# Scale and bias of the exponential moved to VectorE for the last pair of heads, and a tile cleared in six pieces instead of three

## The chip, the cores and the metric

The kernel runs on one core of one Trainium2 chip. The metric is the device time of one execution in microseconds (us), as the median of several runs. A profile of one further execution shows what each engine did. The engines are called TensorE (PE in the profile; its weight loads are PEld), VectorE (DVE), ScalarE (ACT), GpSimd (POOL) and SyncE (SP).

## The reference

Three layers are computed one after the other, all in float32: attention in which a query sees only the keys of its own hash bucket, a mixture of eight experts with one expert for each token, and an ELU feed-forward layer.

```python
# q, k, v: (2, 8, 768, 64); 6 hash bits from the sign of q @ proj and k @ proj
scores = scale * np.matmul(q, k.transpose(0, 1, 3, 2))
scores = np.where(mask, scores, -1000000000.0)
scores = scores - np.max(scores, axis=-1, keepdims=True)
attn = np.exp(scores)
attn = attn / (np.sum(attn, axis=-1, keepdims=True) + 1e-09)
x = np.matmul(attn, v)                      # reshaped to 1536 tokens x 512
logits = x @ w_gate                         # e_idx = argmax; softmax weight of it
eom = 1.0 / (1.0 + np.exp(-(x @ w_output_gate)))
out[mask] = gate_w[mask, None] * eom[mask, e, None] * (np.maximum(x[mask] @ w1[e], 0.0) @ w2[e])
h = out @ w_in                              # 512 x 2048
return np.where(h > 0.0, h, np.exp(np.minimum(h, 0.0)) - 1.0) @ w_out
```

## The kernel before, in words

The order of the instructions on every engine is the order in which the code issues them; nothing reorders them.

The attention is one software pipeline of 96 row blocks (`NQ = 96`): 16 heads in 8 pairs, six blocks of 128 query rows for each head. Step `n` of the loop over `n` issues the stages of several blocks at once, in this order:

- `stage_M(n - 1)`: VectorE reduces the 128x768 scores of block n - 1 in PSUM to the negated row maximum `nm` (L369). GpSimd makes of it the scale `sc` (L370: 2 to the 64th where the row has a key in its bucket, else 0) and the bias `bi = sc * nm` (L371).
- `lows_t`: VectorE forms the low half of the second three transposed tiles of the block before (L405).
- `stage_A(n)`: GpSimd adds up the two halves of an earlier output (L431).
- `early`: what earlier steps have put off, all on VectorE here: the sum into `osb` (L447) for two of the later half heads, and the products of the joining step with the reciprocals of the sums (L509, L528).
- `stage_T(n - 3)`: TensorE transposes the probabilities of block n - 3 in two groups of three (L400) into three PSUM tiles that are used in turn; ScalarE rounds each group to its high half (L402), VectorE subtracts for the low half of the first (L407; the second waits as a `lows_t` for the next step). Between them VectorE may take the reciprocals of sums (L468).
- `stage_G`: GpSimd adds a small constant to the sums (L460).
- `stage_S(n)`: TensorE computes the scores of block n in four matmuls (L351) into one of two PSUM tiles.
- `stage_R`: TensorE joins two heads to token rows (L501).
- `stage_V`: TensorE multiplies the transposed probabilities of three blocks with v, four matmuls a step (L421), into the only PSUM tile `o`.
- `stage_E(n - 1)`: ScalarE computes the exponential with `bi` and `sc` as operands (L378), and with it the row sums.
- `stage_O`: ScalarE copies the finished output out of `o` (L446 and others).
- then whatever the list `todo` holds for step n, put there by `at(n, ...)`.

The last pair of heads are the blocks n = 84 to 95. While they run, the tokens of the first batch element go to their experts: `gate_first` puts its gate arithmetic on the steps 63 to 87 and six scatters (L638, an indirect DMA that GpSimd issues) on the steps 85, 87, 88, 90, 91 and 93. Each is followed on GpSimd by a one-element memset (`spacer`, L651). In step 96 SyncE loads the rows of the first expert.

The tile `zt0` holds zeros. GpSimd clears it early in the pipeline; from step 22 on SyncE writes it to the first rows of each expert's region (`zero_rows`).

Behind the attention come the experts (64 pieces of weights, streamed) and the feed-forward layer; the change touches neither.

Of the kernel before, what the change touches and what calls it, by code (L numbers as in the profile page):

```python
# [13 lines left out]
ALU = mybir.AluOpType  # L14
# [5 lines left out]
UNIT = float(2.0 ** 64)  # L20
# [5 lines left out]
def kernel(  # L26
# [19 lines left out]
    nc = tc.nc  # L46
# [21 lines left out]
    XC = DM + 16  # L68
# [82 lines left out]
    zt0 = ap1.tile([128, XC], F32, name="zt0")  # L151
# [187 lines left out]
    def tile_of(n):  # L339
        m, i = divmod(n, HALF)  # L340
        hd, hf = part_of(m)
        return hd, HALF * hf + i
# [19 lines left out]
    def stage_M(n):  # L362
        hd, c = tile_of(n)
        if c == 0:
            sums[hd] = ap2.tile([128, NC], F32, tag="sums", name="sums", bufs=3)
        nm = ap2.tile([128, 1], F32, tag="nm", name="nm", bufs=3)
        bi = ap2.tile([128, 1], F32, tag="bi", name="bi", bufs=3)
        sc = ap2.tile([128, 1], F32, tag="sc", name="sc", bufs=3)
        nc.vector.tensor_reduce(nm, sps[n][:, :, 0:HC], AX.XY, ALU.max, negate=True)  # L369
        nc.gpsimd.tensor_scalar(sc, nm, 0.25, UNIT, ALU.is_lt, ALU.mult)  # L370
        nc.gpsimd.tensor_tensor(bi, sc, nm, ALU.mult)  # L371
        soft[n] = (bi, sc)

    def stage_E(n):
# [347 lines left out]
    NQ = NH * NC  # L722
# [5 lines left out]
    def at(n, f, *a):  # L728
        todo.setdefault(n, []).append((f, a))
# [37 lines left out]
    for hh in range(2):  # L767
        at(10 + 2 * hh, joining_rows, rw, hh)
        at(14 + 4 * hh, joining_rows, rw_end, hh)
    for j in range(3):  # L770
        at(13 + 3 * j, nc.gpsimd.memset, zt0[:, j * XC // 3:(j + 1) * XC // 3], 0.0)
    for hh in range(2):
        at(12 + 3 * hh, load_gates, hh, False)
        at(61 + 3 * hh, load_gates, hh, True)
# [62 lines left out]
    for pc in range(E * NP):  # L837
        stream.append((pc,))
        j, i = divmod(pc - W2P, 7)
# [165 lines left out]
    for n in range(NQ + 3):  # L1005
# [4 lines left out]
        if 1 <= n < NQ + 1:  # L1010
            stage_M(n - 1)
# [491 lines left out]
```

## Time and profile before

| | us |
|---|---|
| median of 3 runs | 704.16 |
| lowest and highest | 703.58, 704.34 |
| the profiled execution | 704.39 |
| its span from first to last instruction | 702.3 |

The profiled execution took 2.1 us more than its span. TensorE's granted clock was 0.997 of full speed over the span. Durations and times below are from that one execution; times count from the start of the span. An instruction's start to the next one's start is its slot: instructions of an engine overlap a little, so a slot can be shorter than the duration. In a timeline a bracket at the end of a line tells the engine's idle time before it and what ended it.

### The profile page before, as it was taken

The numbers are of one execution on the slowest core, as the hardware profiler recorded it, in microseconds if no ns is written. First come the engines' busy times: TensorE is split into PE (matmuls) and PEld (weight loads), VectorE is DVE, ScalarE is ACT, GpSimd is POOL, SyncE is SP. The second block draws the span as 40 slices with busy tenths as digits, with TensorE's granted clock in tenths as the row PEclk, the third lists the DMA queues.
The fourth block names the chain that finished last, engine by engine and source line by source line (L and its number), as shares of the span: only waits on it lengthen the run. The fifth ranks groups of instructions, "written<-read, shape, count | busy, mean of one in ns | idle before, by whom it ended". The sixth has DMA issues, their size and how long they took to land.

```text
span 702.3 us, 12093 instructions
## 1 busy us (share of the span) xinstructions
PE 688.6 (98%) x4120; PEld 616.4 (88%) x4121; DVE 553.1 (79%) x1026; ACT 427.8 (61%) x854; POOL 214.6 (31%) x503
## 2 busy tenths in 40 slices
PE   8999999999999999999999999999999999999996
PEld 5799999999999989999999998888888888888885
DVE  6999999999999897888888898877788447934433
ACT  5998998999888767666766664444543224422221
POOL 5676556555566640221235410000000000002012
PEclk9999999999999999999999999999999999999998
DMA  8747658667572259777788984222122000001011
GB/s 194 195 115 210 173 161 203 181 174 203 148 201 79 77 184 327 237 244 251 229 211 229 264 218 113 93 88 91 61 90 91 0 1 0 1 1 60 7 53 64
DMA packets 47476, 96.92 MB, mean 138 GB/s; under 512 B 11752, under 2 KB 23848, under 8 KB 47408
## 3 DMA queue, kind: packets, MB, share of 16 engines
q1 hardware_dynamic: 44944, 89.67, 45.2%
q0 software_dynamic: 2304, 6.40, 2.4%
q8 instruction: 35, 0.57, 0.3%
q14 instruction: 33, 0.27, 0.1%
q10 hardware_dynamic: 160, 0.00, 0.0%
HBM read 63.68 MB, written 10.72 MB: 106 GB/s over the span
## 4 chain that ended last, share of the span: by engine, by line
PE 52%; issue 34%; DMA 6%; DVE 5%; ACT 2%; POOL 1%; SPq 0%; DVEq 0%; POOLq 0%; ACTq 0%
PE hps L1186 12%; PE s L351 8%; PE yps L1199 8%; PE o L421 8%; PE t L400 7%; DMA out_dram<-part,tidt 5%; PE yps L1201 3%; PE sp L501 2%; DVE nm L369 2%; PE zps L280 1%; PE xTp L1168 1%; DVE ptlo L407 1%; DMA qb<-qhi 1%; DMA tidt<-tid_d 1%; PE xacc L944 1%
## 5 line engine op out<-in xcount | busy, mean ns | idle before, releaser
L378 ACT ACTIVATE p<-s,bi,sc 128x768 f32<-128x768 f32 x96 | 95.8, 998 | 4.7 <-POOL bi L371 4.3
L886 DVE TENSOR_TENSOR wl<-wraw,wh 128x1024 fp32r<-128x1024 f32 (+1 forms) x65 | 77.2, 1190 | 21.8 <-ACT wh L882 19.6
L1344 POOL DMA_INDIRECT out_dram<-part,tidt x12 | 11.5, 959 | 265.4 <-DVE part L1341 264.2
L369 DVE TENSOR_REDUCE nm<-s 128x1 f32<-128x768 f32 x96 | 90.6, 944 | 2.0 <-POOL vst L330 1.1
L1306 ACT ACTIVATE ee<-gps 128x512 f32<-128x512 f32 x48 | 28.7, 597 | 100.1 <-PE gps L1296 100.1
L402 ACT ACTIVATE pthi<-t 128x384 fp32r<-128x384 f32 x192 | 84.0, 493 | 7.6 <-PE t L400 6.3
L1199 PE MATMUL yps<-h,wh 128*128 128x448 f32 x256 | 84.5, 380 | 0.0
L400 PE MATMUL t<-ident,p 128*128 128x128 f32 x576 | 80.3, 273 | 2.0 <-DVE ptlo L405 1.1
L1296 PE MATMUL gps<-x2l,vh 128*128 128x512 f32 x192 | 75.9, 395 | 0.0
L1326 PE MATMUL a<-vh,gl 128*128 128x512 f32 x192 | 75.8, 395 | 0.0
L1296 PE MATMUL gps<-x2h,vl 128*128 128x512 f32 x192 | 75.7, 394 | 0.0
L1296 PE MATMUL gps<-x2h,vh 128*128 128x512 f32 x192 | 75.7, 394 | 0.0
L1326 PE MATMUL a<-vh,gh 128*128 128x512 f32 x192 | 75.5, 393 | 0.0
L1326 PE MATMUL a<-vl,gh 128*128 128x512 f32 x192 | 75.5, 393 | 0.0
L351 PE MATMUL s<-ka,qa 128*128 128x384 f32 x192 | 73.3, 383 | 1.8 <-DMA qa<-qlo 1.2
L400 PEld LDWEIGHTS t<-ident,p 128*128 128x128 f32 x576 | 68.1, 140 | 7.8 <-PE t L400 1.5
L1307 DVE TENSOR_SCALAR ee<-ee 128x512 f32<-128x512 f32 x48 | 20.4, 426 | 68.0 <-ACT ee L1306 67.9
L1309 ACT ACTIVATE gh<-ee 128x512 fp32r<-128x512 f32 x48 | 30.4, 633 | 69.0 <-DVE ee L1308 69.0
L421 PE MATMUL o<-pthi,vst 128*128 128x384 f32 x192 | 66.9, 348 | 0.3
L882 ACT ACTIVATE wh<-wraw 128x1024 fp32r<-128x1024 f32 x63 | 66.2, 1052 | 0.0
L351 PE MATMUL s<-kb,qb 82*128 82x384 f32 x192 | 65.2, 340 | 0.0
L421 PE MATMUL o<-ptlo,vst 128*128 128x384 f32 x192 | 64.9, 338 | 0.0
(238 smaller groups left out, 1783.9 us busy)
## 6 DMA issues: line engine op xcount, KB each, us to landing
wraw<-in_moe_w_t_dram SPq DMA_DIRECT2D x64, 512.0 KB
w<-in_moe_w_in_dram SPq DMA_DIRECT2D x16, 512.0 KB
w<-in_moe_w_out_dram SPq DMA_DIRECT2D x16, 512.0 KB
ka<-khi SPq DMA_DIRECT2D x30, 192.0 KB
xs_d<-zt SPq DMA_DIRECT2D x8, 528.0 KB
xs<-xs_d SPq DMA_DIRECT2D x7, 462.0 KB
raw_v<-in_v_dram SPq DMA_DIRECT2D x8, 384.0 KB
kb<-klo SPq DMA_DIRECT2D x15, 192.0 KB
```

What stands on the lines that cost most here:

```text
L351: nc.tensor.matmul(ps[:, j, 0:HC], opnd[st, "q" + x][0:n1, cb], opnd[st, "k" + x][0:n1, j * HC:(j + 1) * HC], start=(x == "a"), stop=(x == ...
L369: nc.vector.tensor_reduce(nm, sps[n][:, :, 0:HC], AX.XY, ALU.max, negate=True)
L378: nc.scalar.activation(p.rearrange("p (a b) -> p a b", a=2), sps.pop(n)[:, :, 0:HC], AF.Exp, bias=bi, scale=sc, accum_out=sums[hd][:, c:c ...
L400: nc.tensor.transpose(ps[:, a, :], p[:, kt * 128:(kt + 1) * 128], ident)
L402: nc.scalar.activation(ho, ps, AF.Copy)
L421: nc.tensor.matmul(ops[m], vst[hd][:, kt, :], t[:, kt, :], start=(kt == 0 and x == 0), stop=(kt == NC - 1 and x == 1))
L882: eng_hi.activation(hi, r, AF.Copy)
L886: fs = [lambda c=slice(j, j + h): eng.tensor_tensor(lo[:, c], r[:, c], hi[:, c], ALU.subtract) for j in range(0, PW, h)]
L1186: nc.tensor.matmul(ps, w[:, dc, fs], x[:, dc], start=(i == 0), stop=(i == len(terms) - 1))
L1199: nc.tensor.matmul(ps, wh[:, f], h[:, :, f], start=(f == 0), stop=last)
L1296: nc.tensor.matmul(ps, w[:, dc], x[:, dc, th * TC:(th + 1) * TC], start=(dc == 0 and i == 0), stop=(dc == KD - 1 and i == 2),)
L1326: nc.tensor.matmul(ps, x[:, cs], w, start=(fb in first_fb and i == 0), stop=(fb in last_fb and i == 2))
```

## The change

Two edits. In `stage_M` the engine of the scale and of the bias is VectorE where n is 84 or more, and GpSimd as before elsewhere. The arithmetic is the same. The tile `zt0` (528 columns) is cleared in six pieces of 88 columns at steps 11, 12, 14, 15, 17 and 18, instead of three of 176 columns at steps 13, 16 and 19.

```diff
         nc.vector.tensor_reduce(nm, sps[n][:, :, 0:HC], AX.XY, ALU.max, negate=True)
-        nc.gpsimd.tensor_scalar(sc, nm, 0.25, UNIT, ALU.is_lt, ALU.mult)
-        nc.gpsimd.tensor_tensor(bi, sc, nm, ALU.mult)
+        eng = nc.vector if n >= NQ - 12 else nc.gpsimd
+        eng.tensor_scalar(sc, nm, 0.25, UNIT, ALU.is_lt, ALU.mult)
+        eng.tensor_tensor(bi, sc, nm, ALU.mult)
         soft[n] = (bi, sc)
...
-    for j in range(3):
-        at(13 + 3 * j, nc.gpsimd.memset, zt0[:, j * XC // 3:(j + 1) * XC // 3], 0.0)
+    for j in range(6):
+        at(11 + 3 * j // 2, nc.gpsimd.memset, zt0[:, j * XC // 6:(j + 1) * XC // 6], 0.0)
```

## Rows read from the trace of the kernel before

**Rows 1.** The page: the span, and each engine's busy time
```profile
span 702.3 us, 12093 instructions
PE 688.6 (98%) x4120; PEld 616.4 (88%) x4121; DVE 553.1 (79%) x1026; ACT 427.8 (61%) x854; POOL 214.6 (31%) x503
```

**Rows 2.** Windows: length, then busy us (instructions) by engine, clock, DMA share, GB/s
```profile
30.00:60.00 30.00, 30.00 (x201) 28.99 (x200) 28.14 (x52) 28.38 (x63) 21.30 (x64) 1.00 0.62 153
...
210.00:220.00 10.00, 9.87 (x65) 9.25 (x64) 9.49 (x18) 8.95 (x21) 7.38 (x20) 1.00 0.16 60
```

**Rows 3.** Waits, 209 to 235 us: total us, times, longest
```profile
PEld o L421 <- DVE osb L447: 0.9, 2, 0.5
...
ACT p L378 <- POOL bi L371: 0.3, 1, 0.3
PEld s L351 <- ACT p L378: 0.2, 1, 0.2
```

**Rows 4.** Chain of waits in order of time: start us, us, what
```profile
211.47 1.22 POOL xs_d L638
...
213.35 1.08 ACT p L378 x2
...
214.97 0.57 DVE osb L447
...
218.27 1.07 POOL xs_d L638
...
224.56 0.82 PE sp L501 x6
```

**Rows 5.** Timeline of TensorE: start us, us, engine, line, operation, out<-in
```profile
210.17 0.42 PE L351 MATMUL s<-ka,qa 128*128 128x384 f32 x1
...
212.25 0.42 PE L351 MATMUL s<-ka,qa 128*128 128x384 f32 x1
...
215.12 0.34 PE L351 MATMUL s<-kb,qb 82*128 82x384 f32 x1
215.58 0.44 PE L421 MATMUL o<-pthi,vst 128*128 128x384 f32 x1
```

**Rows 6.** Timeline of VectorE, the last pair of heads
```profile
209.25 0.95 DVE L369 TENSOR_REDUCE nm<-s 128x1 f32<-128x768 f32 x1
...
215.56 0.56 DVE L407 TENSOR_TENSOR ptlo<-t,pthi 128x384 fp32r<-128x384 f32 x1
216.03 0.95 DVE L369 TENSOR_REDUCE nm<-s 128x1 f32<-128x768 f32 x1
216.90 0.55 DVE L405 TENSOR_TENSOR ptlo<-t,pthi 128x384 fp32r<-128x384 f32 x1
...
225.53 0.55 DVE L405 TENSOR_TENSOR ptlo<-t,pthi 128x384 fp32r<-128x384 f32 x1
225.99 0.25 DVE L509 TENSOR_TENSOR lp<-sp,ri 128x96 f32<-128x96 f32 x1
226.15 0.55 DVE L528 TENSOR_TENSOR xw<-sp,ri 128x384 f32<-128x384 f32 x1
...
234.56 0.93 DVE L369 TENSOR_REDUCE nm<-s 128x1 f32<-128x768 f32 x1
```

**Rows 7.** Timeline of VectorE, the last gate
```profile
247.18 0.18 DVE L622 TENSOR_REDUCE g_zs<-g_oz 128x3 f32<-128x24 f32 x1
247.28 0.17 DVE L618 TENSOR_REDUCE g_se<-g_ed 128x3 f32<-128x24 f32 x1
247.48 0.31 DVE L620 TENSOR_SCALAR g_se<-g_se 128x3 f32<-128x3 f32 x1
```

**Rows 8.** Timeline of GpSimd, the first piece of the tile of zeros
```profile
41.37 0.24 POOL L1040 MEMSET zt<- 128x176 f32 x1
```

**Rows 9.** Timeline of GpSimd, a scatter beside the last gate
```profile
246.85 0.96 POOL L638 DMA_INDIRECT xs_d<-xw,g_idx  x1 [0.21 <-issue]
```

**Rows 10.** Groups by line on VectorE: busy us, mean ns, then idle before
```profile
L620 DVE TENSOR_SCALAR g_se<-g_se 128x3 f32<-128x3 f32 x2 | 0.5, 232 | 0.0
```


## The prediction

> **What bounds the kernel now.** I first read the page's busy shares. TensorE is busy 688.6 of 702.3 us, VectorE 553.1, GpSimd only 214.6 [rows 1]. So GpSimd can cost time only where something waits for it in line, and work given to VectorE is free only where VectorE has gaps. The whole-run average doesn't say whether it has any here. I therefore read the windows of the last pair of heads, whose twelve row blocks (n = 84 to 95) are reduced from 209.25 us on. In 210 to 220 us VectorE is busy 9.49 of 10 us and TensorE 9.87 [rows 2]. Two engines are nearly full at once. The reader should see that the engine that is to be relieved (GpSimd, 7.38 of 10) is the emptiest of the three, and that the work goes to one of the full ones.
>
> The table of waits for 209 to 235 us prices what GpSimd does wrong there: ScalarE's exponential waits for `bi` once, 0.3 us; TensorE then waits 0.2 us for the exponential, and twice, 0.9 us together, for the combined output `osb` (L447) [rows 3]. The chain of waits shows that these belong together: a scatter of 1.22 us at 211.47, behind it in GpSimd's queue the scale and bias, then the exponential at 213.35, then `osb` at 214.97; the same again behind the scatter at 218.27 [rows 4]. On TensorE's side the last matmul of L351 starts at 215.12 and takes 0.34, and the first of L421 starts only at 215.58, with the end of `osb` at 215.54 [rows 4, 5]. So what the change can win is 0.9 + 0.2 = 1.1 us, 0.15% of the run. About 0.2% (1.4 us) is what a measurement of this kernel can tell from no change; a gain alone can't reach it.
>
> **The change, part by part.** *The twelve pairs on VectorE.* For n = 84 to 95 the scale (L370) and the bias (L371) run on VectorE directly behind the reduction (L369), and ahead of all that the step issues there: the low halves of the turned probabilities (L405, L407), the sum into `osb` (L447), the reciprocals (L468) and the products of the joining step (L509, L528). What the two instructions take is slots in that queue.
>
> The slots of a step before the change, start to next start where nothing is waited for [rows 6]: the reduction 0.87 (216.03 to 216.90), L405 0.46 (225.53 to 225.99), L407 0.47 (215.56 to 216.03). A plain step needs 0.87 + 0.46 + 0.47 = 1.80 us of VectorE. A plain step of TensorE is 2.08 (212.25 less 210.17) [rows 5]. So VectorE has 0.28 us left in a plain step.
>
> The new slots aren't in the trace; the nearest rows are the gate's chain of small instructions [rows 7]. L618 starts 0.10 after L622, whose result it doesn't read. L620 reads L618's result and starts 0.20 after it, which is L618's own 0.17 plus 0.03. The scale reads the reduction and the bias reads the scale, so I take the dependent price for both; the next instruction (L405) reads neither and gets the independent one. The reduction then holds the queue for its whole 0.95 + 0.03 instead of 0.87, the scale 0.20, the bias 0.10: 1.28 in place of 0.87, or 0.41 more for each block. The bounds: two independent slots and no lost overlap, 0.20 for each block; upward, each scale held by a GpSimd instruction (a rival, below). I take 0.41 because the two dependences are in the code and the row is of the same operation, three columns instead of one.
>
> Now the sum for the eleven steps from the reduction of n = 84 (209.25) to that of n = 95 (234.56) [rows 6], 25.31 us:
> - TensorE needs 11 x 2.08 = 22.9 and two joining products at 0.82 [rows 4] = 24.5; the other 0.8 are the stalls above.
> - VectorE needs 11 x 1.80 = 19.8; L447 twice at L407's slot, 0.94; two joining steps at 0.16 (L509, 225.99 to 226.15) + 0.47 (L528, as L407), 1.26; four reciprocals at 0.10, 0.4. That is 22.4, so 2.9 us are free.
> - After the change VectorE needs 11 x 0.41 = 4.5 more: 26.9, which is 1.6 more than the stretch has now and 2.4 more than TensorE needs.
> - The twelfth block (n = 95) lies behind 234.56, where VectorE's low half and TensorE's joining step follow directly: 0.41 more.
>
> So the stretch goes from bound by TensorE to bound by VectorE and ends 1.6 + 0.4 = 2.0 us later. What is late next: L405 and L407 release the three PSUM tiles of the transposes, so TensorE waits for them; L447 releases the only `o` tile, so the two waits that were to go can stay, now because L447 stands behind the bias; and every following reduction starts late. GpSimd loses 24 short instructions and issues its six scatters earlier. No one gains: their rows are first read by the load of the first expert's rows on SP's queue in step 96, and the last of these scatters belongs to step 93. The exponential gets its bias sooner after a reduction, but the reductions themselves come later by more than that after a step or two.
>
> *The tile of zeros in six pieces.* Three memsets of 128x176 at 0.24 us, the first at 41.37 [rows 8], become six of 128x88. Between half of 0.24 and all of it, that is 0 to 0.7 us more of GpSimd in all, at steps 11, 12, 14, 15, 17 and 18 instead of 13, 16 and 19: from two steps ahead of the one at 41.37 to five behind it. In 30 to 60 us GpSimd is busy 21.30 of 30 and TensorE 30.00 of 30 [rows 2], so what may be delayed by a piece is hidden by TensorE's own work. I cost it at nothing; were the cover gone, the bound is the 0.7. The loads that read the tile are issued from step 22 on, so its end at step 18 instead of 19 frees no one.
>
> **Sum.** The profiled execution took 704.39 us (span 702.3 and 2.1 around it), 0.23 over the median of 704.16. It would take 706.4; against the median 706.2. TensorE is the bound of the whole run at 98% [rows 1], so I take it that nothing later gives the 2.0 us back.
>
> **The rivals.** *A, forecast:* VectorE becomes the bound, 1.4 to 2.6 us slower (705.6 to 706.8).
>
> *B, the short price:* the slots cost nearer to 0.3 than 0.41, since one column is shorter than three and part of the wait overlaps. Then 11 x 0.3 = 3.3 less the 2.9 free and one block of 0.3 behind: +0.7 us, 704.9, within 0.2%. For it: the independent rows at 0.10 [rows 7]. Against it: L620 waited out L618.
>
> *C, the other side:* VectorE's gaps cover the new slots and GpSimd's wait goes. The place is the pair of chains through the scatters at 211.47 and 218.27 [rows 4], the price the 1.1 us above: 703.1 us at best, 704.2 where L447's wait stays. It decides the case if a block adds less than 2.9 / 11 = 0.26 us to VectorE. For it: the trace does run its chain through those scatters. Against it: 0.26 is near the lowest bound of 0.20, and the gaps don't lie where the slots are put.
>
> *D, a collision of the scale with GpSimd:* the scale is a tensor_scalar from SBUF to SBUF on VectorE, and six scatters of about 1.1 us still run on GpSimd in the same 25 us. The one row that shows such a pair: L620 began at 247.48 inside a scatter (246.85 to 247.81) [rows 7, 9], took 0.31 and ended within 0.02 of the scatter's end; its mean of two is 232 ns, so the other took 0.15 [rows 10]. A collision thus costs 0.15 as seen, at most a whole scatter. Six scatters fill a quarter of the stretch, so about three of twelve scales meet one; at 0.15 to half a scatter each, 0.5 to 1.6 us on top of A: 706.7 to 707.8. Against it: L937, issued behind that L620, started 0.07 us later.
>
> The Trainium skill has this as a rule (SBUF — State Buffer, Who interferes with whom): VectorE's copies and tensor_scalars from SBUF in a two-port mode and GpSimd's instructions take one shared port pair, and the second to start waits for the whole of the first. The L620 row agrees with it; whether one column per partition takes that mode no row here shows. By the rule the sum would be that of D, without it that of A.
>
> **How the numbers follow.** A 0.50, B 0.22, C 0.16 (a quarter of it below 702.8, by gains that I don't see), D 0.12. Slower by over 0.2% is A and D: 0.62. Faster by over 0.2% is 0.04. Within it is B and the rest of C: 0.34. The range from 703.9 to 707.6 leaves out the lower half of C and the upper part of D, 0.12 in all; A and B alone would give 704.6 to 706.8. The predicted time is A's, 706.2.
>
> **What would show it.** Right: the time from the reduction of n = 84 to that of n = 95 grows from 25.31 to about 27 us; VectorE is busy over 9.7 of 10 there; reduction to L405 is 1.28 instead of 0.87; TensorE waits for L405, L407 or L447 in most steps; the chain of waits no longer goes through the scatters but through VectorE. Wrong: scale and bias together under 0.26 a block, or VectorE with gaps at unchanged step times (C); scales of 0.3 us and more beside scatters (D); or a difference that stands already at 209 us, which would be the memsets' doing.

## The result and the profile after

The changed kernel takes 708.06 us (707.52 to 708.31, 6 runs) against 703.87 (703.5 to 704.34, 6 runs) for the kernel before: a ratio of 1.0058, 95% interval 1.0045 to 1.0071, 3.2 to 5.0 us slower. The forecast was slower, 706.2, with a range up to 707.6; the direction came out and the size was twice the forecast. The profiled execution has a span of 706.2 us.

The page's span and the window of [rows 1, 2], after the change:

```profile
span 706.2 us, 12079 instructions
```
```profile
210.00:220.00 10.00, 8.89 (x60) 8.40 (x59) 9.66 (x23) 8.31 (x19) 5.95 (x11) 1.00 0.27 109
```

VectorE is busier than before (9.66 of 10 us for 9.49), GpSimd emptier (5.95 for 7.38), and TensorE has fallen from 9.87 to 8.89. So in the last pair of heads the bound went from TensorE to VectorE.

The timeline of VectorE (start us, us, engine, line, operation), of which [rows 6] is the counterpart; from here on L406 to L529 are what was L405 to L528 before:

```profile
208.52 0.95 DVE L369 TENSOR_REDUCE nm<-s 128x1 f32<-128x768 f32 x1
209.51 0.15 DVE L371 TENSOR_SCALAR sc<-nm 128x1 f32<-128x1 f32 x1
209.69 0.16 DVE L372 TENSOR_TENSOR bi<-sc,nm 128x1 f32<-128x1 f32 x1
209.77 0.55 DVE L406 TENSOR_TENSOR ptlo<-t,pthi 128x384 fp32r<-128x384 f32 x1
210.24 0.55 DVE L408 TENSOR_TENSOR ptlo<-t,pthi 128x384 fp32r<-128x384 f32 x1
...
214.48 0.55 DVE L406 TENSOR_TENSOR ptlo<-t,pthi 128x384 fp32r<-128x384 f32 x1
215.06 0.56 DVE L448 TENSOR_TENSOR osb<-o,osb 64x384 f32<-64x384 f32 x1
215.65 0.56 DVE L408 TENSOR_TENSOR ptlo<-t,pthi 128x384 fp32r<-128x384 f32 x1
...
227.50 0.55 DVE L529 TENSOR_TENSOR xw<-sp,ri 128x384 f32<-128x384 f32 x1
228.03 0.56 DVE L408 TENSOR_TENSOR ptlo<-t,pthi 128x384 fp32r<-128x384 f32 x1
228.50 0.17 DVE L469 RECIPROCAL ri<-sm 128x3 f32<-128x3 f32 x1
228.83 0.96 DVE L369 TENSOR_REDUCE nm<-s 128x1 f32<-128x768 f32 x1 [0.15 <-PE s L351]
...
237.26 0.96 DVE L369 TENSOR_REDUCE nm<-s 128x1 f32<-128x768 f32 x1 [0.16 <-PE s L351]
```

The reader should see three things. From the reduction of n = 84 (208.52) to that of n = 95 (237.26) it is now 28.74 us where it was 25.31: 3.43 more. The reduction's slot is 1.25 (208.52 to 209.77) for 0.87; from the reduction to the low half the four instructions follow each other with pauses of at most 0.04 us. And in the joining steps VectorE itself waits, 0.15 us before 228.83, for the scores of TensorE, which are late because TensorE waited for VectorE in the steps before.

From the reduction of n = 95 to the first matmul of the experts it was 20.16 us (234.56 to 254.72) and is now 20.95 (237.26 to 258.21): 0.79 more. Together 4.2 us, which is the whole difference of the medians. (The spans of the two profiles differ by 3.9 us: the changed one stood 0.7 ahead at n = 84, see below, and took 0.4 longer behind these matmuls.) The rows of these first matmuls, of the kernel before and of the changed one:

```profile
254.72 0.34 PE L1186 MATMUL hps<-xt,wh 128*128 128x224 f32 x1
```
```profile
258.21 0.34 PE L1187 MATMUL hps<-xt,wh 128*128 128x224 f32 x1
```

The changed kernel's profile stood 0.73 us ahead at n = 84 (208.52 for 209.25). That arose at the fourth reduction, near 16 us, ahead of which VectorE sat idle for 1.10 us in the profile before and not in the one after. It lies ahead of the first piece of the tile of zeros in either kernel, and profiles without the six pieces have it too (208.56 with two blocks on VectorE, below). It is no part of the change.

Of the table of waits, 205 to 245 us (total us, times, longest), the lines that answer to [rows 3]:

```profile
PEld o L422 <- DVE osb L448: 2.6, 2, 1.4
...
PE sp L502 <- DVE ptlo L406: 1.9, 2, 1.0
```

The two waits for `osb` didn't go: they grew from 0.9 to 2.6 us. Two waits of the joining matmuls for the low half came to 1.9 us, where the kernel before had one of 0.2. The chain of waits from 208 to 239 us now has nothing of GpSimd in it; where it ran through two scatters [rows 4] it runs down VectorE's queue:

```profile
211.87 0.44 DVE bi L372
...
222.37 0.57 DVE osb L448
...
222.99 0.98 PE o L422 x4
```

One thing in it wasn't in the forecast: two biases, of 0.44 us (211.87) and 1.00 us (232.19). The next view gives all twelve scales and biases on VectorE (shortest, median and longest ns):

```profile
L371 DVE TENSOR_SCALAR sc<-nm x12: 153/154/154, 209.5 to 238.2; 128x1 f32<-128x1 f32 x12
L372 DVE TENSOR_TENSOR bi<-sc,nm x12: 159/160/1004, 209.7 to 238.4; 128x1 f32<-128x1 f32 x12
```

Every scale took 0.15; nine biases took 0.16 and three did not. Their rows on VectorE, with one bias that wasn't held and one scale for comparison:

```profile
211.87 0.44 DVE L372 TENSOR_TENSOR bi<-sc,nm 128x1 f32<-128x1 f32 x1
...
217.29 0.16 DVE L372 TENSOR_TENSOR bi<-sc,nm 128x1 f32<-128x1 f32 x1
...
232.19 1.00 DVE L372 TENSOR_TENSOR bi<-sc,nm 128x1 f32<-128x1 f32 x1
...
238.25 0.15 DVE L371 TENSOR_SCALAR sc<-nm 128x1 f32<-128x1 f32 x1
238.44 0.54 DVE L372 TENSOR_TENSOR bi<-sc,nm 128x1 f32<-128x1 f32 x1
```

and what GpSimd did at the same times:

```profile
211.27 1.02 POOL L432 TENSOR_TENSOR osb<-o,o 64x384 f32<-64x384 f32 x1
...
216.46 1.04 POOL L639 DMA_INDIRECT xs_d<-xw,g_idx  x1 [0.28 <-issue]
...
232.14 1.04 POOL L885 CAST wh<-wraw 128x1024 fp32r<-128x1024 f32 x1
...
236.43 2.52 POOL L887 TENSOR_TENSOR wl<-wraw,wh 128x512 fp32r<-128x512 f32 x2
```

The three end where a GpSimd instruction ends: 212.31 and the addition L432 at 212.29, 233.19 and the cast L885 at 233.18, 238.98 and the two subtractions L887 at 238.95. The bias at 217.29 ran inside a scatter and wasn't held, and neither were the scales at 211.69, inside L432, and at 238.25, inside L887. Held time: 0.28 + 0.84 + 0.38 = 1.5 us, 1.12 of it before n = 95.

### The profile page after: what moved, and what is told of

It is laid out like the page before. It is cut to its first block, busy times and chain, and to the rows that moved or that the text cites. A ratio compares the mean times of both kernels' runs of the same rounds, so it can differ in the third digit from the quotient of the medians.

```text
span 706.2 us, 12079 instructions
## 1 busy us (share of the span) xinstructions
PE 689.1 (98%) x4120; PEld 615.9 (87%) x4121; DVE 557.3 (79%) x1050; ACT 428.3 (61%) x854; POOL 209.3 (30%) x482
## 4 chain that ended last, share of the span: by engine, by line
PE 51%; issue 34%; DVE 7%; DMA 6%; ACT 1%; POOL 1%; SPq 1%; DVEq 0%; ACTq 0%; POOLq 0%
PE hps L1187 12%; PE yps L1200 8%; PE s L351 8%; PE o L422 7%; PE t L401 7%; DMA out_dram<-part,tidt 5%; PE yps L1202 3%; DVE nm L369 2%; PE sp L502 2%; PE zps L280 1%; DVE ptlo L406 1%; DVE ptlo L408 1%; PE xTp L1169 1%; PE xacc L945 1%; DMA tidt<-tid_d 1%
## 5 line engine op out<-in xcount | busy, mean ns | idle before, releaser
L887 DVE TENSOR_TENSOR wl<-wraw,wh 128x1024 fp32r<-128x1024 f32 (+1 forms) x65 | 77.1, 1189 | 21.9 <-ACT wh L883 20.2
```

Of the source, the lines that this page charges most:

```text
L887: fs = [lambda c=slice(j, j + h): eng.tensor_tensor(lo[:, c], r[:, c], hi[:, c], ALU.subtract) for j in range(0, PW, h)]
```

## The experiments

Every comparison is with runs of the kernel before on the same chip.

**The move alone.** The first hunk of the diff without the second.

> Only the move of scale and bias to VectorE for the blocks n = 84 to 95; the tile of zeros in three pieces as before. Theory (the move is all of it): 4.2 us over the kernel before, the reductions of n = 84 and n = 95 again some 28.7 us apart instead of 25.3. Rival (the six pieces have a share): less than 3.5 us over before.

708.11 us, ratio 1.0059 (1.0046 to 1.0073): as slow as the whole change. From n = 84 to n = 95 it is 28.75 us (208.85 to 237.60), and the same three biases are held.

**The six pieces alone.** The second hunk without the first.

> Only the six pieces of the tile of zeros; scale and bias on GpSimd throughout. Theory: within 0.5 us of the kernel before, 25.3 us between the reductions of n = 84 and n = 95. Rival (the pieces delay the pipeline, or gain the 0.7 us by which the changed kernel stood ahead at 209 us): 0.5 us or more either way, and the step times from n = 10 to 20 differ.

704.43 us, ratio 1.0009 (1.0000 to 1.0018), and 25.35 us from n = 84 to n = 95 (208.59 to 233.94). The 0.5 us by which the medians differ lies outside the span: the span has a median of 701.8 us in these runs and in those of the kernel before, and what comes on top of it is 2.4 to 3.0 us here and 2.0 to 2.2 there. The changed kernel, which has the same pieces, has 2.0 to 2.2 as well; the cause stays open. The steps 10 to 20 are as long as in the other profiles. With the move alone as slow as the whole change, the pieces have no share that can be seen.

**The bias with one tensor input.** In the changed kernel:

```diff
-        eng.tensor_tensor(bi, sc, nm, ALU.mult)
+        if eng is nc.vector:
+            eng.tensor_scalar(bi, nm, sc, None, ALU.mult)
+        else:
+            eng.tensor_tensor(bi, sc, nm, ALU.mult)
```

> The changed kernel, with the bias on VectorE written as a tensor_scalar of nm with sc as the scalar of each partition, in place of a tensor_tensor of sc and nm: the same product with one tensor input. Theory (three biases were held because a tensor_tensor with two inputs in SBUF can't run beside a GpSimd instruction that reads SBUF): no bias over 0.2 us, 1.5 us less than the changed kernel, so 2.7 over before; the distance from n = 84 to n = 95 about 27.6 us. Rival (any VectorE instruction that meets a GpSimd addition or cast is held): still about three biases of 0.4 to 1.0 us, no gain over the changed kernel.

707.07 us, ratio 1.0048 (1.0034 to 1.0061): 1.0 less than the changed kernel, not 1.5. All twelve biases take the same time, also beside the same GpSimd instructions; in this kernel L432 is L435 and L885 is L888. Its biases, two of them in VectorE's timeline, and GpSimd's timeline at their times:

```profile
L373 DVE TENSOR_SCALAR bi<-nm,sc x12: 214/214/215, 210.0 to 238.2; 128x1 f32<-128x1 f32 x12
```
```profile
212.26 0.21 DVE L373 TENSOR_SCALAR bi<-nm,sc 128x1 f32<-128x1 f32 x1
212.39 0.55 DVE L409 TENSOR_TENSOR ptlo<-t,pthi 128x384 fp32r<-128x384 f32 x1
...
232.69 0.21 DVE L373 TENSOR_SCALAR bi<-nm,sc 128x1 f32<-128x1 f32 x1
```
```profile
211.61 1.02 POOL L435 TENSOR_TENSOR osb<-o,o 64x384 f32<-64x384 f32 x1
...
232.59 1.04 POOL L888 CAST wh<-wraw 128x1024 fp32r<-128x1024 f32 x1
```

So it was the form with two tensor inputs that was held, and the theory stands; whether the second input makes it or another trait of the tensor_tensor, no run separates. The missing 0.5 us is the new form's own price: its slot is 0.13 (212.26 to 212.39) where that of the two-input bias is 0.08, 0.05 more in each of twelve blocks, 0.6. The stretch takes 28.15 us (208.86 to 237.01).

**Two more instructions on VectorE, nothing taken from GpSimd.** The kernel before, with

```diff
         nc.gpsimd.tensor_tensor(bi, sc, nm, ALU.mult)
+        if n >= NQ - 12:
+            da, db = (ap2.tile([128, 1], F32, tag=x, name=x, bufs=3) for x in ("da", "db"))
+            nc.vector.tensor_scalar(da, nm, 0.25, UNIT, ALU.is_lt, ALU.mult)
+            nc.vector.tensor_scalar(db, nm, da, None, ALU.mult)
```

and a second kernel with `da` alone. Nothing reads what they compute.

> As the run before with two more instructions, a scale and a bias with one tensor input each that nothing reads; the ones that are used stay on GpSimd. Theory (VectorE's queue alone makes the loss, and what GpSimd is spared gains nothing): 28.0 us from n = 84 to n = 95, about 3 us over before, as with the used ones on VectorE with one tensor input (3.2 over). Rival (the move has a gain on GpSimd's side that the loss hides): 4 us or more over before.

706.65 us, ratio 1.0042 (1.0027 to 1.0058), 28.16 us from n = 84 to n = 95. This is the stretch of the run above to 0.01 us, though here GpSimd still does the work and issues its scatters late. Nothing that GpSimd was spared gave time.

> The kernel before, scale and bias on GpSimd as they were, and one more instruction on VectorE behind the reduction of each of the blocks n = 84 to 95: a second scale that nothing reads. Theory (each block has some 0.26 us of VectorE free, and one dependent instruction takes about that much): 25.3 to 25.9 us from n = 84 to n = 95, 0 to 0.7 us over before. Rival (every slot on VectorE costs its length from the first): 11 or 12 times 0.25, about 3 us more.

704.35 us, ratio 1.0009 (1.0000 to 1.0019), 25.77 us: 0.46 more. One dependent instruction in each block nearly fits, two don't. The four reductions, n = 84 and n = 95, first with two more and then with one more:

```profile
208.12 0.95 DVE L369 TENSOR_REDUCE nm<-s 128x1 f32<-128x768 f32 x1
...
236.28 0.96 DVE L369 TENSOR_REDUCE nm<-s 128x1 f32<-128x768 f32 x1 [0.21 <-PE s L351]
```
```profile
208.61 0.95 DVE L369 TENSOR_REDUCE nm<-s 128x1 f32<-128x768 f32 x1
...
234.38 0.96 DVE L369 TENSOR_REDUCE nm<-s 128x1 f32<-128x768 f32 x1
```

**Two blocks on VectorE.** The kernel before, with VectorE for n = 85 and 88 only, whose scales stood behind the scatters of [rows 4]:

```diff
+        eng = nc.vector if n in (NQ - 11, NQ - 8) else nc.gpsimd
```

and the one-input bias.

> The kernel before, with scale and bias on VectorE in two blocks only, n = 85 and n = 88, whose GpSimd instructions stood behind the scatters of the chain; the bias with one tensor input. Theory (the slots cost because there are twelve of them; the wait for GpSimd is worth up to 1.1 us and lies in these two): two slots of 0.38 fit into VectorE's gaps, 0.3 to 1.1 us less than before. Rival (a slot costs its full length wherever it stands): 0.5 to 0.8 us more than before.

703.9 us, ratio 1.0002 (0.9993 to 1.0011), 25.41 us from n = 84 to n = 95. By the stretch both theory and rival missed: no gain, no loss. The exponential came earlier, but the sum into `osb` (L451 here) didn't gain from it. ScalarE's timeline and then the chain of waits:

```profile
213.39 0.48 ACT L450 ACTIVATE osb<-o 64x384 f32<-64x384 f32 x1
```
```profile
212.94 0.84 DVE nm L369
213.79 0.46 DVE ptlo L409
...
214.28 0.57 DVE osb L451
```

ScalarE's half was ready at 213.87; VectorE came to the sum at 214.28, behind a reduction and a low half that the two added slots had moved back.

**The scatters elsewhere, and the sum first.** Three kernels more asked whether the 1.1 us can be had at all. One moves the scatters away from the steps in which GpSimd has most to do:

```diff
-        for n, f in zip((85, 87, 88, 90, 91, 93), scs):
+        for n, f in zip((86, 87, 89, 90, 92, 93), scs):
```

> The kernel before, with the six scatters put on the steps 86, 87, 89, 90, 92 and 93 in place of 85, 87, 88, 90, 91 and 93, away from the steps in which GpSimd also adds to the sums; scale and bias stay on GpSimd. Theory (as the two blocks on VectorE showed, the sum into osb then waits in VectorE's own queue behind the reduction and the low half): no bias waits for a scatter on the chain, yet within 0.4 us of before; 25.3 us from n = 84 to n = 95. Rival (the scatters cost the 1.1 us that the waits show): 0.7 to 1.1 us less.

703.65 us, ratio 0.9997 (0.9988 to 1.0006), 25.18 us (208.82 to 234.00): the theory's case. Its chain of waits has no scatter in it; the sum into `osb` at 214.28 follows VectorE's own reduction (212.94) and low half (213.79). The next puts the sum ahead of the low half, with the two blocks on VectorE kept:

```diff
+        now, early[:] = early[:], []
+        if n in (NQ - 9, NQ - 6):
+            both(now)
+            now = []
         both(lows_t)
         lows_t.clear()
         stage_A(n)
-        now, early[:] = early[:], []
         both(now)
```

> The kernel with two blocks (n = 85 and 88) on VectorE, and in the steps 87 and 90 the sum into osb issued on VectorE ahead of the low half instead of behind it. Theory (GpSimd's wait and VectorE's order hold TensorE in turn, so that both have to go): the two waits of TensorE for osb fall from 0.5 us to under 0.2 each, 0.5 to 0.8 us less than before. Rival (something else ends last): within 0.3 us of before.

703.78 us, ratio 0.9999 (0.9990 to 1.0008), 25.26 us. The theory fell. The waits for `osb` did shrink, from 0.9 to 0.4 us, but the exponential now waited 0.7 us for its bias (0.3 before), and the chain of waits shows TensorE's matmuls taking longer in other places, the scores 0.97 us for a usual 0.71 and the joining step 1.05 for 0.82. The wait for `osb` (209 to 235 us), then the chain:

```profile
PEld o L425 <- DVE osb L451: 0.4, 2, 0.3
```
```profile
218.07 0.97 PE s L351 x4
...
223.43 1.05 PE sp L505 x6
```

The same order with the scatters moved and VectorE left alone:

> The kernel before with the scatters on the steps 86, 87, 89, 90, 92 and 93, and in the steps 87 and 90 the sum into osb ahead of the low half on VectorE; no slot is added to VectorE and none of GpSimd's is moved to it. Theory (both waits gone, VectorE as before): 24.6 to 24.9 us from n = 84 to n = 95, 0.4 to 0.7 us less than before. Rival (the pipeline is balanced: TensorE's small waits come back at other places, as with two blocks on VectorE and the sum first, 25.26 us): within 0.3 us of before.

703.82 us, ratio 0.9998 (0.9989 to 1.0007), 25.43 us (208.72 to 234.15): the rival's number, but not a test of its reason. The theory's "both waits gone" didn't come about: with the sum first, the exponential waited 0.9 us for its bias (209 to 235 us), and a scatter is back on the chain of waits:

```profile
ACT p L378 <- POOL bi L371: 0.9, 3, 0.4
```
```profile
213.40 1.22 POOL xs_d L638
...
215.26 1.09 ACT p L378 x2
```

And the order alone:

> The kernel before with only the order changed: in the steps 87 and 90 the sum into osb ahead of the low half on VectorE. Theory (the sum waited for ScalarE, 0.3 us, and so for GpSimd; an earlier place can't start it earlier, and the low half now waits behind it): the same or up to 0.5 us more than before. Rival (its place in VectorE's queue was what held TensorE): 0.4 to 0.8 us less.

704.68 us, ratio 1.0011 (1.0002 to 1.0020), 26.17 us (208.64 to 234.81): 0.8 us slower, by somewhat more than the theory's 0.5. VectorE stood still for ScalarE's half and the exponential for GpSimd, as its waits show (209 to 236 us):

```profile
DVE osb L447 <- ACT osb L446: 1.6, 2, 0.8
ACT p L378 <- POOL bi L371: 1.5, 4, 0.5
```

No kernel of the study is faster than the one before by more than its interval.

## Why the prediction was right and wrong

**The mechanism was right.** The bound went to VectorE; the reductions and not the scatters carry the chain; the waits for `osb` stayed for the reason given, the sum's place behind the bias. The two unread instructions show it without any change on GpSimd. The memsets cost nothing that can be seen, as forecast.

**The slot was a little too high.** 0.41 was forecast for each block. Measured is 1.25 less 0.87, 0.38, and 4.1 in place of 4.5 for eleven blocks.

**The sum of VectorE's other slots was too low by 0.6.** L447 was put at L407's slot of 0.47, twice. It takes 0.59 (215.06 to 215.65), and the low half ahead of it 0.58 (214.48 to 215.06) where 0.46 was put: 0.24 in each of two steps. The 0.59 could have been read before the change: L447 at 214.97 and L407 behind it at 215.56 [rows 4, 6]. From L528 (now L529) to the next low half it is 0.53 for 0.47 (227.50 to 228.03), 0.06 twice.

**That VectorE would run without a gap was wrong by 0.5.** In the two joining steps it waits for TensorE: from the reciprocal at 228.50 to the reduction at 228.83 it is 0.33 in place of 0.09. The forecast took the larger of the two engines' sums as the bound; but each engine also waited for the other in turn, and what VectorE lost in those two steps came on top of its sum.

These make 1.6 - 0.4 + 0.6 + 0.5 = 2.3 for the stretch, and 3.43 less the 1.12 of held biases is 2.31.

**The step that failed is the collision with GpSimd, which the sum put at nothing.** Rival D put it on the scale, beside a scatter, at 0.15 us as seen, with a chance of 0.12, and left it out of the sum. The scale never collided, with a scatter or anything else. The bias did, with GpSimd's addition, cast and subtractions, for 0.28, 0.84 and 0.38 us: as long as those instructions still had to run. That is 1.5 of the 2.2 us by which the forecast was short; the three terms above make the other 0.7. The forecast looked for a row of the first new instruction (a tensor_scalar) and never asked for one of the second (a tensor_tensor of two tiles in SBUF); and it listed the scatters, and not the rest of GpSimd's queue in that stretch.

The trace of the kernel before shows such a pair the other way round. GpSimd's bias takes 0.19 there in the last pair of heads, but up to 0.58 in earlier ones, where VectorE had just begun a subtraction of two tiles in SBUF; here it ends 0.05 after that (21.30 and 21.25):

```profile
20.70 0.55 DVE L222 SCALAR_TENSOR_TENSOR qlo<-raw_q,qhi 128x384 fp32r<-128x384 f32 x1
```
```profile
20.73 0.57 POOL L371 TENSOR_TENSOR bi<-sc,nm 128x1 f32<-128x1 f32 x1
```

The Trainium skill would have told scale and bias apart: the page quoted in the prediction (SBUF — State Buffer, Who interferes with whom) says in the same section that a VectorE instruction with two inputs in SBUF meets a GpSimd instruction that reads SBUF, and not one that only writes it. The traces agree with the first half beside GpSimd's addition L432, its cast L885 and its subtractions L887. Beside its tensor_scalar L912 they don't: that ran on tiles in SBUF from 240.65 to 243.78, and a VectorE addition of two tiles in SBUF took 0.25 in the middle of it, as it did elsewhere (0.26 at 248.84); one more instruction with two such inputs took 0.40 for 0.18 (242.54) and was done 0.84 before L912 ended. After the change, VectorE and then GpSimd:

```profile
241.80 0.25 DVE L515 TENSOR_TENSOR lg<-lg,lp 128x96 f32<-128x96 f32 x1
```
```profile
240.65 3.13 POOL L912 TENSOR_SCALAR xs<-xs 128x512 f32<-128x512 f32 x2
```

So the measured rule is narrower than the page's. The second half no run tests: two biases weren't held inside a scatter (217.29 and 224.61), but a scatter has the row numbers `g_idx` as an input, and whether GpSimd reads them from SBUF while it runs no row shows. The one-input form was held nowhere.

The twelfth block was forecast at 0.4 behind the stretch and took 0.79: its slot of 0.38 and a held bias of 0.38.

**Rival C's price was reached by no kernel either.** The 1.1 us was read as what TensorE lost to GpSimd, though the prediction's own sum left only 0.8 us for TensorE's stalls. Four kernels (two blocks on VectorE, moved scatters, and each with the sum first) moved the stretch between 25.18 and 25.43 us, against 25.31; only the last of them still had a scatter on its chain. TensorE's weight loads waited 1.2, 0.7, 0.4 and 0.5 us for `osb` in them, for 0.9 before, and ScalarE's exponential waited for its bias not at all in the table of the first, then 0.5, 0.7 and 0.9 us, for 0.3 before: where the one wait shrank, the other grew. Which waits would have to go together to gain the 1.1 us was not found.

## What to carry to other kernels

Before work goes to a second engine to spare a first one, sum the slots of one step on the second, each read between the same neighbours as in the code, and compare them with the step: here 0.28 us were free, one instruction nearly fitted and two did not. Look up both inputs of each moved instruction as well as its length: a product of two tiles in SBUF on VectorE stood still until GpSimd's addition, cast or subtraction was done, the same product with the factor as a scalar operand didn't; and neither a scatter nor a tensor_scalar on GpSimd held an instruction with two inputs until its end. A wait in the table is what an engine stood still for, not what the kernel gains without it.

## What the runs showed of the hardware

A tensor_scalar on VectorE with one column in each partition wasn't held by GpSimd in any run: 153 to 154 ns for all twelve scales, the one inside L887 among them, and 214 to 215 ns with the factor as a scalar operand from SBUF. A tensor_tensor of one column was held up to 0.84 us beyond its 0.16, by a cast of GpSimd until that ended. GpSimd's tensor_scalar L912 held a VectorE instruction with two inputs in SBUF by 0.22 us at most (0.40 for 0.18 at 242.54). And the slot of an instruction depends on its neighbours. The low half L406 takes 0.47 before another low half (209.77 to 210.24) and 0.58 before the sum into `osb`, which starts 0.03 after the low half's end (215.03), as the next low half starts 0.03 after the sum's (215.62). ScalarE's half of the sum was done at 214.00. The sum reads and writes partitions 64 to 127, the low halves all 128. The Trainium skill has a model of this (VectorE: DVE Perf Modes, Two Vector instructions with no wait between them): an instruction whose input starts in another quarter of the partitions than the last one read from that memory starts only when all earlier ones are done. Both starts agree with it; no run here changed the partitions to test it.
